# Another order of the first instructions of a fused attention and SwiGLU kernel

## The chip, the cores and the metric

The kernel runs on one core of one Trainium2 chip. The metric is the device time of one execution in microseconds (us), lower is better; the number before is the median of five runs.

## The reference

Attention with normalised queries and keys over 8 sequences and 12 heads of 448 tokens and 64 columns, and then a SwiGLU feed-forward block over the 3584 x 768 matrix that the heads make side by side:

```python
def rmsnorm(x, g):
    return x / np.sqrt(np.mean(x * x, axis=-1, keepdims=True) + 1e-06) * g
q_n, k_n = rmsnorm(q, g_q), rmsnorm(k, g_k)
scores = np.matmul(q_n, k_n.transpose(0, 1, 3, 2)) / np.sqrt(64)
attn = softmax(scores)                        # over the keys
x = np.matmul(attn, v)                        # (8, 12, 448, 64) -> (3584, 768)
xn = rmsnorm(x, rms_g)
g, val = xn @ w_gate, xn @ w_val              # 768 x 1536 each
out = (g * sigmoid(g) * val) @ w_out          # 1536 x 768
```

## The kernel before, in words

**Pairs.** Two heads make a pair; there are 6 pairs for each sequence and 48 in all, and pair `g` is the unit of the attention part. The 448 tokens of a head are cut into three blocks of 128 (`FULL`, handled as [128 partitions, 3 blocks]) and 64 last ones, the *rest*. The rests of all 12 heads of a sequence lie in one tile `rest`: queries in 64 of its partitions, keys in the other 64.

**One pair.** `load_pair` brings q in one DMA and k in two into the tile `qk`; `load_rests` brings the rests' queries (i = 0) or keys (i = 1) in two DMAs each. `squares(g, i)` squares the queries (i = 0) or keys (i = 1) on ScalarE (ACT, L478) and sums them by row on VectorE (DVE, L481). `rms_qk` makes the reciprocal roots on GpSimd (POOL): an addition (L497) and a power (L498). `norm_q` scales the queries into the tile `qn` (L503, two instructions). The keys are not scaled; their root goes into the exponential as a scale by row. `norm_rests(b, lo, hi)` does the same for the rests of pairs lo to hi: square on ACT (L446), sum on DVE (L448), root on POOL (L453, L454), scale (L458).

`turn(g, 0)` transposes the queries on TensorE (PE, L519, three instructions) and the rest tile (L523), and copies the result to `qT` with ACT (L524) and to the last 64 columns of `kT` with DVE (L525). `turn(g, 1)` transposes the keys (L519) and copies them to the first 384 columns of `kT` with DVE (L527). `score(g, cs)` multiplies (L537) and takes exponentials on ACT (L541) for the key blocks in `cs`, `rests(g)` for the rest keys (L567, L582). `values(g)` makes the products with v in the PSUM bank `av` (L573, L589), `sums(g)` the softmax denominators: for the first seven pairs directly on PE (L578, L602), followed by a reciprocal (L606, 2.95 us) and the product `x` (L617) on DVE. `av` has a single bank, so that the next pair's L573 follows this pair's L617.

**Weights.** They come as 64-bit numbers and are made 32-bit ones piece by piece: `convert()` moves each piece one step on, with a load on SP's queue (L719), a split on ACT (L728, L729), a join on DVE (L734, L735, L736; called a conversion below), an addition on POOL (L773) and a store (L761). Conversions start with the second pair. From about 100 us on the feed-forward products fill PE beside the attention of the next sequences.

**The order.** It is written out by hand: each engine and each DMA queue takes its instructions in the order in which the Python code issues them, and semaphores hold an instruction until its inputs are there. `pe(fn)` issues a block of PE work and counts it; `after(n, fn)` puts other work on a list, to be issued when n more blocks have been counted:

```python
def pe(fn):
    now["t"] += 1
    fn()
    for item in [d for d in due if d[0] <= now["t"]]:
        due.remove(item)
        item[1]()
```

Work that falls due at the same block is issued in the order in which it was put on the list. `warm(n)` issues n products of the identity with itself, whose result nothing reads; each shows as two records in the trace.

Of the kernel before, what the change touches and what calls it, by code (L numbers as in the profile page):

```python
# [8 lines left out]
F32 = mybir.dt.float32  # L9
# [3 lines left out]
ALU = mybir.AluOpType  # L13
ACT = mybir.ActivationFunctionType
AX_X = mybir.AxisListType.X
# [3 lines left out]
B, H, S, D = 8, 12, 448, 64  # L19
DM, DF = H * D, 1536  # L20
NT, P = 4, 112
NK, REST = 3, S - 3 * 128
# [313 lines left out]
def safe_scores(  # L336
# [20 lines left out]
    nc = tc.nc  # L357

    def pool(name, bufs, **kw):
        return ctx.enter_context(tc.tile_pool(name=name, bufs=bufs, **kw))  # L360
# [3 lines left out]
    qk_pool, v_pool, qn_pool, qkT_pool = pool("c_qk", 4), pool("c_v", 3), pool("c_qn", 1), pool("c_qkT", 2)  # L364
# [9 lines left out]
    st = {}  # L374
# [4 lines left out]
    def after(n, fn):  # L379
        due.append((now["t"] + n, fn))  # L380
# [7 lines that stand above are left out]
# [12 lines left out]

    FULL, LAST = slice(0, NK * 128), slice(NK * 128, S)

    def load_pair(g):

        if g >= NG:
            return
        b, hp = divmod(g, NPAIR)
        qk = st["qk", g] = qk_pool.tile([128, 2, 2 * NK * D], F32, name="qk")
        nc.sync.dma_start(out=qk[:, 0].rearrange("p (h n) -> p h n", h=2),
                          in_=q[b, 2 * hp:2 * hp + 2, FULL].rearrange("h (p t) d -> p h (t d)", t=NK))  # L410
        for h in range(2):
            nc.sync.dma_start(out=qk[:, 1].rearrange("p (t h d) -> p h t d", h=2, d=D)[:, 1 - h],
                              in_=k[b, 2 * hp + h, FULL].rearrange("(p t) d -> p t d", t=NK))

# [9 lines left out]
    def load_rests(b, i, engine):  # L424
        if b >= B:
            return
        if i == 0:
            st["rest", b] = rest_pool.tile([128, NPAIR, 2, D], F32, name="rest")
        for h in range(2):
            engine.dma_start(out=st["rest", b][own(i), :, 1 - h], in_=(q, k)[i][b, h::2, LAST].rearrange("h i d -> i h d"))  # L430
# [8 lines left out]
    def norm_rests(b, lo, hi):  # L439

        if b >= B:
            return
        n = hi - lo
        rest = st["rest", b][:, lo:hi]
        sq = tmp.tile([128, n, 2, D], F32, name="sq", tag="sq", bufs=2)
        nc.scalar.activation(sq, rest, ACT.Square)  # L446
        ms = small.tile([128, n, 2], F32, name="msr")
        after(1, lambda: nc.vector.tensor_reduce(out=ms, in_=sq, axis=AX_X, op=ALU.add))  # L448

        first = b == lo == 0  # L450

        def root():
            nc.gpsimd.tensor_scalar(ms, ms, D * 1e-6, None, ALU.add)  # L453
            nc.gpsimd.tensor_tensor(ms, ms, mhalf[:, 0:2 * n].rearrange("p (n h) -> p n h", h=2), ALU.pow)  # L454

        def scale():

            (nc.vector if first else nc.gpsimd).tensor_tensor(rest, rest, ms.unsqueeze(3).to_broadcast([128, n, 2, D]), ALU.mult)  # L458

        after(1 if b == 0 else 2, root)  # L460
        if first:
            return scale
        after(1 if b == 0 else 2, scale)

    def direct(g):
# [3 lines left out]
    def squares(g, i):  # L469

        if g >= NG:
            return
        n = 2 * NK
        if i == 0:
            st["ms", g] = small.tile([128, 2 * n], F32, name="ms")
        ms = st["ms", g]
        sq = tmp.tile([128, n * D], F32, name="sq", tag="sq", bufs=2)
        nc.scalar.activation(sq, st["qk", g][:, i], ACT.Square)  # L478

        def reduce():  # L480
            nc.vector.tensor_reduce(out=ms[:, i * n:(i + 1) * n], in_=sq.rearrange("p (n d) -> p n d", d=D), axis=AX_X, op=ALU.add)  # L481

        after(1, reduce)
        if g <= 1:

            after(1, lambda: rms_qk(g, slice(i * n, (i + 1) * n)))
            if i == 0:
                after(1, lambda: norm_q(g))
        elif i == 1:
            after(2, lambda: rms_qk(g))  # L490
            after(2, lambda: norm_q(g))

    def rms_qk(g, cols=slice(0, 4 * NK)):
        if ("rs", g) not in st:
            st["rs", g] = small.tile([128, 4 * NK], F32, name="rs")
        ms = st["ms", g][:, cols]
        nc.gpsimd.tensor_scalar(ms, ms, D * 1e-6, None, ALU.add)  # L497
        nc.gpsimd.tensor_tensor(st["rs", g][:, cols], ms, mhalf[:, cols], ALU.pow)  # L498

    def norm_q(g):  # L500
        qn = st["qn", g] = qn_pool.tile([128, 2 * NK * D], F32, name="qn")
        for h in range(2):
            (nc.vector if g <= 1 else nc.gpsimd).tensor_tensor(  # L503
                qn.rearrange("p (t h d) -> p h t d", h=2, d=D)[:, 1 - h], st["qk", g][:, 0].rearrange("p (h t d) -> p h t d", h=2, d=D)[:, h],
                st["rs", g][:, h * NK:(h + 1) * NK].unsqueeze(2).to_broadcast([128, NK, D]), ALU.mult)

# [669 lines left out]
        todo.extend(items + (out_items(b) if b == B - 1 else []))  # L1176


    load_pair(0)
    load_rests(0, 0, nc.scalar)  # L1180
    load_rests(0, 1, nc.sync)
    load_pair(1)
    ident = const.tile([128, 128], F32, name="ident")
    make_identity(nc, ident)
# [20 lines left out]
    def gains():  # L1205


        nc.vector.scalar_tensor_tensor(gqk, gq, D**0.5, gk, ALU.mult, ALU.mult)
        nc.vector.tensor_scalar(gqk, gqk, SAFE, -SAFE, ALU.min, ALU.max)
# [28 lines left out]
            convert()  # L1238


    squares(0, 0)
    warm(9)
    pe(idle)
    scale = norm_rests(0, 0, 2)
    squares(0, 1)
    after(1, scale)
    pe(lambda: turn(0, 1))
    gains()
    squares(1, 0)
    squares(1, 1)  # L1250
    warm(5)
    pe(lambda: turn(0, 0))
    for g in range(NG + 1):
        b, hp = divmod(g, NPAIR)
        if g:
            load_pair(g + 3)
        if hp == 2:
            for i in range(2):
                load_rests(b + 1, i, nc.sync)
            load_v_rests(b + 1)  # L1260
        if g == 0:
            pe(lambda: score(0, (0,)))
            pe(lambda: rests(0))
            pe(lambda: score(0, (1, 2)))
            pe(lambda: turn(1, 0))
            squares(2, 0)
            squares(2, 1)
            pe(lambda: turn(1, 1))
            norm_rests(0, 2, 4)
            for _ in range(3):  # L1270
                convert()
            load_pair(3)
            load_v(2)
            convert()
            load_rows()
            continue
        if g <= NPAIR:
            pe(lambda: score(g, (0,)))
            squares(g + 2, 0)
            squares(g + 2, 1)  # L1280
            turns(g < NPAIR)
            if g > 1:
                pe(lambda: turn(g + 1, 0))
                some_rests(g)
                pe(lambda: turn(g + 1, 1))
            pe(lambda: rests(g))
            pe(lambda: values(g - 1))
            if g == 1:
                pe(lambda: turn(g + 1, 0))
                some_rests(g)  # L1290
                pe(lambda: turn(g + 1, 1))
            load_v(g + 2)
            turns(g < NPAIR)
            pe(lambda: sums(g - 1))
            pe(lambda: score(g, (1, 2)))
            turns(1 if g < NPAIR else 3)
            if g == 2:
                bound()
            continue

        pe(lambda: (rests(g), score(g, (0,)) if g < NG else None))
        if g == NPAIR + 1:
            pe(lambda: rms_x(0))
        pe(lambda: values(g - 1))
        load_v(g + 2)
        if g == NPAIR + 1:
            pe(lambda: score(g, (1,)))
            pe(lambda: norm_x(0))
            pe(lambda: score(g, (2,)))
        pe(lambda: sums(g - 1))  # L1310
        if g == NPAIR + 1:
            begin(0, 15)
        elif g < NG:
            pe(lambda: score(g, (1, 2)))
        st["block"] = now["t"]
        if hp:
            fill()
            squares(g + 2, 0)
            squares(g + 2, 1)
            pe(lambda: turn(g + 1, 0))  # L1320
            some_rests(g)
            fill()
            pe(lambda: turn(g + 1, 1))
            fill()
            continue
        fill(3)
        pe(lambda: turn(g + 1, 0))
        fill(1)
        pe(lambda: rms_x(b - 1))
        squares(g + 2, 0)  # L1330
        squares(g + 2, 1)
        pe(lambda: turn(g + 1, 1))
        fill(len(todo))
        begin(b - 1, 16)
        pe(lambda: norm_x(b - 1))
        fill()
# [41 lines left out]
```

## Time and profile before

| | |
|---|---|
| median of 5 runs | 1604.63 us (1603.41 to 1605.05) |
| the profiled execution | 1601.5 us |
| its span, first to last instruction | 1599.7 us |
| PE busy | 1572.5 us, 98% |
| DVE, POOL, ACT busy | 879.4, 658.8, 469.9 us |
| granted TensorE clock | 0.999 |

A row of the order of time reads: start in us, length in us, engine, line of the kernel, operation, output <- input, shapes, how many instructions were merged, and in brackets the idle time of the engine ahead of it with what ended it. PEld is TensorE's loading of weights, SPq the DMA queue of SyncE. A row of busy time by stretches reads: start:end, length, busy time of the engine with the number of instructions, granted TensorE clock, share of the DMA engines, GB/s. The lengths of PE's records are modelled, and records of one engine overlap a little; sums are therefore made from start to start where an instruction follows another.

### The profile page before, as it was taken

The page shows a single profiled execution, that of the slowest core. Times are in us where ns is not written, and L with a number is a line of the kernel's source. Part 1 is how long each engine was busy: PE and PEld are TensorE (multiplying, and loading weights), DVE is VectorE, ACT ScalarE, POOL GpSimd, SP SyncE. Part 2 cuts the span into 40 slices and gives each one's busy share as a digit, 9 for nine tenths or more (in the row PEclk, how much of TensorE's full clock was granted, in tenths as well). Part 3 has the DMA queues.
Part 4 walks back from the last instruction along what each step waited for, and adds up shares of the span by engine and source line. Part 5 has one row for each costly group of instructions (what it writes and reads, how often), then busy time and mean ns, then how long its engine had stood idle before and what let it go on. Part 6 is the DMA issues. An engine that isn't in the chain of part 4 may idle for free.

```text
span 1599.7 us, 21577 instructions
## 1 busy us (share of the span) xinstructions
PE 1572.5 (98%) x7286; PEld 1114.3 (70%) x7286; DVE 879.4 (55%) x1553; ACT 469.9 (29%) x940; POOL 658.8 (41%) x715
## 2 busy tenths in 40 slices
PE   8999999999999999999999999999999999999998
PEld 4344445687756887568875788667885688859974
DVE  5989899578833556325562354635563355513531
ACT  6746464232222222222222222323322222101010
POOL 7867877465424443343433443344542342000000
PEclk9999999999999999999999999999999999999999
DMA  7648574866756554465544755584553544457652
GB/s 216 199 139 264 165 242 134 278 196 222 250 160 195 154 150 134 134 202 153 155 122 137 208 154 154 149 261 129 163 149 124 173 141 136 124 167 218 174 150 60
DMA packets 261996, 273.28 MB, mean 171 GB/s; under 512 B 78836, under 2 KB 258804, under 8 KB 261876
## 3 DMA queue, kind: packets, MB, share of 16 engines
q1 hardware_dynamic: 260948, 271.61, 56.6%
q8 instruction: 60, 0.98, 0.3%
q14 instruction: 60, 0.49, 0.1%
q10 hardware_dynamic: 800, 0.20, 0.1%
q0 software_dynamic: 128, 0.00, 0.0%
HBM read 232.40 MB, written 39.32 MB: 170 GB/s over the span
## 4 chain that ended last, share of the span: by engine, by line
PE 79%; DVE 7%; issue 1%; POOL 0%; DMA 0%; ACT 0%; SPq 0%; DVEq 0%; POOLq 0%
PE ff L889 40%; PE ff L1079 22%; PE sc L537 6%; PE av L589 5%; PE sc L567 2%; PE den L602 2%; PE tr L519 1%; DVE top L735 1%; DVE top L736 1%; DVE top L734 1%; PE ff L989 1%; DVE rd L610 1%; DVE h L912 0%; DVE h L911 0%; DVE w L846 0%
## 5 line engine op out<-in xcount | busy, mean ns | idle before, releaser
L889 PE MATMUL ff<-x,w 128*128 128x224 f32 x1878 | 381.5, 354 | 4.4 <-DVE h L912 2.6
L889 PEld LDWEIGHTS ff<-x,w 128*128 128x128 f32 x1878 | 351.3, 190 | 20.0 <-issue 11.1
L547 POOL TENSOR_TENSOR es<-e 128x448 f32<-128x448 f32 x82 | 91.6, 1138 | 495.3 <-ACT e L541 495.3
L889 PE MATMUL ff<-xs,w 128*128 128x224 f32 x1374 | 281.7, 353 | 3.3 <-DVE w L846 3.3
L889 PEld LDWEIGHTS ff<-xs,w 128*128 128x128 f32 x1374 | 258.0, 190 | 7.1 <-issue 6.0
L554 POOL TENSOR_TENSOR es<-es,e 64x448 f32<-64x448 f32 (+1 forms) x164 | 191.8, 1180 | 6.3
L610 DVE RECIPROCAL rd<-rd 128x448 f32<-128x448 f32 x41 | 121.0, 2952 | 110.5 <-ACT rd L609 110.5
L541 ACT ACTIVATE e<-sc,rs 128x448 f32<-128x448 f32 x288 | 161.6, 634 | 48.0 <-PE sc L537 45.6
L1079 PE MATMUL ff<-w,h 128*128 128x384 f32 x498 | 167.8, 487 | 0.6 <-ACT p L1058 0.6
L1079 PE MATMUL ff<-w,raw 128*128 128x384 f32 x468 | 159.5, 487 | 0.3 <-DVE y L1051 0.3
L537 PE MATMUL sc<-qT,kT 64*128 64x448 f32 x576 | 138.4, 572 | 3.4 <-ACT sq L478 1.8
L1079 PEld LDWEIGHTS ff<-w,h 128*128 128x128 f32 x498 | 93.5, 190 | 64.5 <-issue 1.3
L1079 PEld LDWEIGHTS ff<-w,raw 128*128 128x128 f32 x468 | 87.6, 190 | 60.9 <-issue 2.6
L589 PE MATMUL av<-e,vt 128*64 128x448 f32 x576 | 118.8, 548 | 0.0
L498 POOL TENSOR_TENSOR rs<-ms,mhalf 128x12 f32<-128x12 f32 (+1 forms) x50 | 114.2, 2283 | 4.2
L537 PEld LDWEIGHTS sc<-qT,kT 64*128 64x128 f32 x576 | 54.4, 185 | 84.4 <-issue 68.3
L1107 PE MATMUL ff<-x,w 128*128 128x448 f32 x288 | 111.8, 541 | 0.0
L901 DVE TENSOR_TENSOR cc<-ff,u 128x448 f32<-128x448 f32 x84 | 52.4, 623 | 91.8 <-PE ff L889 91.6
L773 POOL TENSOR_TENSOR w<-top,raw 128x384 int32<-128x384 int32 x72 | 77.4, 1088 | 36.5 <-DVE top L736 20.0
L589 PEld LDWEIGHTS av<-e,vt 128*64 128x64 f32 x576 | 37.1, 136 | 75.6 <-issue 74.9
L1107 PEld LDWEIGHTS ff<-x,w 128*128 128x128 f32 x288 | 53.3, 190 | 50.8 <-issue 49.0
L623 POOL TENSOR_TENSOR ss<-ss,rd 128x448 f32<-128x448 f32 x40 | 46.9, 1172 | 79.5 <-ACT rd L622 79.5
(127 smaller groups left out, 1809.9 us busy)
## 6 DMA issues: line engine op xcount, KB each, us to landing
w<-kept SPq DMA_DIRECT2D x511, 192.0 KB, 2.7
w<-kept_o SPq DMA_DIRECT2D x296, 192.0 KB, 2.7
kept<-w SPq DMA_DIRECT2D x89, 192.0 KB, 3.9
qk<-in_q_dram SPq DMA_DIRECT2D x48, 192.0 KB, 3.1
qk<-in_k_dram SPq DMA_DIRECT2D x96, 96.0 KB, 3.5
vt<-in_v_dram SPq DMA_DIRECT2D x48, 192.0 KB, 2.5
raw<-in_moe_w_gate_dram SPq DMA_DIRECT2D x24, 384.0 KB, 4.5
raw<-in_moe_w_val_dram SPq DMA_DIRECT2D x24, 384.0 KB, 4.8
```

Of the source, the lines that this page charges most:

```text
L498: nc.gpsimd.tensor_tensor(st["rs", g][:, cols], ms, mhalf[:, cols], ALU.pow)
L537: nc.tensor.matmul(ps[:, 0:S], lhsT=kT[r, c * 128:(c + 1) * 128], rhs=qT[r, :], start=True, stop=True)
L541: nc.scalar.activation(e, ps[:, 0:S], ACT.Exp, scale=rs[:, n:n + 1])
L547: nc.gpsimd.tensor_tensor(es, st["e", g, 0, j], st["e", g, 1, j], ALU.add)
L554: nc.gpsimd.tensor_tensor(es[r], es[r], e[r], ALU.add)
L589: nc.tensor.matmul(av[own(j), 0:S], lhsT=vt[:, j, c], rhs=st["e", g, c, j], start=False, stop=(c == NK - 1), skip_group_check=True)
L610: nc.vector.reciprocal(rd, rd)
L773: nc.gpsimd.tensor_tensor(data(key).bitcast(I32), top, lo, ALU.add)
L889: nc.tensor.matmul(bank[:, w * HT:(w + 1) * HT], lhsT=wt[:, c * 128:(c + 1) * 128], rhs=x[:, c, :], start=onto is None and w == c == 0, st ...
L901: nc.vector.tensor_tensor(add[name], ps[:, 0:S], add[other], ALU.add)
L1079: nc.tensor.matmul(ps, lhsT=left_o(b, which, LEFT_O[name], c), rhs=data(("wo", b, name, c)), start=first and c == 0, stop=c == NFP - 1, sk ...
L1107: nc.tensor.matmul(bank[w][:, 0:S], lhsT=data(key)[:, c * 128:(c + 1) * 128], rhs=st["x", 0, half][:, c, :], start=half == c == 0, stop=ha ...
```

## The change

Only the order of the first three pairs and the engine of two of their steps change; nothing that is computed changes.

- **Loads.** On SP's queue the keys of the first rests go ahead of the first pair's k (two DMAs each). The queries of the rests stay on ACT's queue.
- **First steps.** `squares` of pairs 0 and 1 and `norm_rests(0, 0, 2)` hand back their sum and root, and these are issued by name where they stand, no longer by the list. VectorE's order becomes: sum of q0, `norm_q(0)`, sum of the rests, copy of the keys (L527), sum of k0, scale of the rests, gains, sum of q1, copy of the rest keys (L525), sum of k1, `norm_q(1)`. An empty `pe(idle)` goes.
- **First scores.** `score(0, (1, 2))` is cut in two, and `turn(1, 0)` stands between them. The number of counted blocks is the same as before, so that everything later falls due at the same places.
- **Third pair.** `norm_q(2)` moves from POOL to DVE, and so does the scaling of the rests of pairs 2 and 3 (L458).

```diff
--- before.py
+++ after.py
@@ -400,15 +400,17 @@
 
     FULL, LAST = slice(0, NK * 128), slice(NK * 128, S)
 
-    def load_pair(g):
+    def load_pair(g, parts=(0, 1)):
 
         if g >= NG:
             return
         b, hp = divmod(g, NPAIR)
-        qk = st["qk", g] = qk_pool.tile([128, 2, 2 * NK * D], F32, name="qk")
-        nc.sync.dma_start(out=qk[:, 0].rearrange("p (h n) -> p h n", h=2),
-                          in_=q[b, 2 * hp:2 * hp + 2, FULL].rearrange("h (p t) d -> p h (t d)", t=NK))
-        for h in range(2):
+        if 0 in parts:
+            qk = st["qk", g] = qk_pool.tile([128, 2, 2 * NK * D], F32, name="qk")
+            nc.sync.dma_start(out=qk[:, 0].rearrange("p (h n) -> p h n", h=2),
+                              in_=q[b, 2 * hp:2 * hp + 2, FULL].rearrange("h (p t) d -> p h (t d)", t=NK))
+        qk = st["qk", g]
+        for h in range(2) if 1 in parts else ():
             nc.sync.dma_start(out=qk[:, 1].rearrange("p (t h d) -> p h t d", h=2, d=D)[:, 1 - h],
                               in_=k[b, 2 * hp + h, FULL].rearrange("(p t) d -> p t d", t=NK))
 
@@ -445,21 +447,24 @@
         sq = tmp.tile([128, n, 2, D], F32, name="sq", tag="sq", bufs=2)
         nc.scalar.activation(sq, rest, ACT.Square)
         ms = small.tile([128, n, 2], F32, name="msr")
-        after(1, lambda: nc.vector.tensor_reduce(out=ms, in_=sq, axis=AX_X, op=ALU.add))
-
+        reduce = lambda: nc.vector.tensor_reduce(out=ms, in_=sq, axis=AX_X, op=ALU.add)
         first = b == lo == 0
+
+        engine = nc.vector if b == 0 and lo < 4 else nc.gpsimd
 
         def root():
             nc.gpsimd.tensor_scalar(ms, ms, D * 1e-6, None, ALU.add)
             nc.gpsimd.tensor_tensor(ms, ms, mhalf[:, 0:2 * n].rearrange("p (n h) -> p n h", h=2), ALU.pow)
 
         def scale():
-
-            (nc.vector if first else nc.gpsimd).tensor_tensor(rest, rest, ms.unsqueeze(3).to_broadcast([128, n, 2, D]), ALU.mult)
-
+            engine.tensor_tensor(rest, rest, ms.unsqueeze(3).to_broadcast([128, n, 2, D]), ALU.mult)
+
+        if first:
+            reduce()
+            root()
+            return scale
+        after(1, reduce)
         after(1 if b == 0 else 2, root)
-        if first:
-            return scale
         after(1 if b == 0 else 2, scale)
 
     def direct(g):
@@ -480,13 +485,11 @@
         def reduce():
             nc.vector.tensor_reduce(out=ms[:, i * n:(i + 1) * n], in_=sq.rearrange("p (n d) -> p n d", d=D), axis=AX_X, op=ALU.add)
 
+        if g <= 1:
+
+            return reduce, lambda: rms_qk(g, slice(i * n, (i + 1) * n))
         after(1, reduce)
-        if g <= 1:
-
-            after(1, lambda: rms_qk(g, slice(i * n, (i + 1) * n)))
-            if i == 0:
-                after(1, lambda: norm_q(g))
-        elif i == 1:
+        if i == 1:
             after(2, lambda: rms_qk(g))
             after(2, lambda: norm_q(g))
 
@@ -500,7 +503,7 @@
     def norm_q(g):
         qn = st["qn", g] = qn_pool.tile([128, 2 * NK * D], F32, name="qn")
         for h in range(2):
-            (nc.vector if g <= 1 else nc.gpsimd).tensor_tensor(
+            (nc.vector if g <= 2 else nc.gpsimd).tensor_tensor(
                 qn.rearrange("p (t h d) -> p h t d", h=2, d=D)[:, 1 - h], st["qk", g][:, 0].rearrange("p (h t d) -> p h t d", h=2, d=D)[:, h],
                 st["rs", g][:, h * NK:(h + 1) * NK].unsqueeze(2).to_broadcast([128, NK, D]), ALU.mult)
 
@@ -1176,9 +1179,10 @@
         todo.extend(items + (out_items(b) if b == B - 1 else []))
 
 
-    load_pair(0)
+    load_pair(0, (0,))
     load_rests(0, 0, nc.scalar)
     load_rests(0, 1, nc.sync)
+    load_pair(0, (1,))
     load_pair(1)
     ident = const.tile([128, 128], F32, name="ident")
     make_identity(nc, ident)
@@ -1238,18 +1242,26 @@
             convert()
 
 
-    squares(0, 0)
+    def at_once(steps):
+        for step in steps:
+            step()
+
+    at_once(squares(0, 0))
     warm(9)
-    pe(idle)
+    norm_q(0)
     scale = norm_rests(0, 0, 2)
-    squares(0, 1)
-    after(1, scale)
+    steps = squares(0, 1)
     pe(lambda: turn(0, 1))
+    at_once(steps)
+    scale()
     gains()
-    squares(1, 0)
-    squares(1, 1)
+    at_once(squares(1, 0))
+    reduce, root = squares(1, 1)
     warm(5)
     pe(lambda: turn(0, 0))
+    reduce()
+    norm_q(1)
+    root()
     for g in range(NG + 1):
         b, hp = divmod(g, NPAIR)
         if g:
@@ -1261,8 +1273,9 @@
         if g == 0:
             pe(lambda: score(0, (0,)))
             pe(lambda: rests(0))
-            pe(lambda: score(0, (1, 2)))
+            pe(lambda: score(0, (1,)))
             pe(lambda: turn(1, 0))
+            pe(lambda: score(0, (2,)))
             squares(2, 0)
             squares(2, 1)
             pe(lambda: turn(1, 1))
```

## The prediction

> **What bounds the kernel now.** I read the page first, then busy time by stretches, then the order of time of each engine over the first 100 us.
>
> ```profile
> span 1599.7 us, 21577 instructions
> PE 1572.5 (98%) x7286; PEld 1114.3 (70%) x7286; DVE 879.4 (55%) x1553; ACT 469.9 (29%) x940; POOL 658.8 (41%) x715
> ```
>
> PE is idle for 27 us in all, so no order of instructions can bring more, and the change reaches only what runs before about 35 us. PE's own order of time has three pauses at the places that are edited:
>
> ```profile
> 10.00 0.33 PE L523 MATMUL tr<-ident,rest 128*128 128x128 f32 x1 [1.10 <-DVE rest L458]
> 17.56 1.02 PE L537 MATMUL sc<-qT,kT 64*128 64x448 f32 x4 [1.82 <-ACT sq L478]
> 24.29 0.33 PE L523 MATMUL tr<-ident,rest 128*128 128x128 f32 x1 [1.16 <-POOL rest L458]
> ```
>
> They are 4.08 us together. But from 25 us on another engine has no room either. Busy time of VectorE by stretches (start:end, length, busy):
>
> ```profile
> 20.00:25.00 5.00, 1.19 (x3) 1.00 0.54 158
> 25.00:30.00 5.00, 4.61 (x7) 1.00 0.97 264
> 30.00:40.00 10.00, 9.76 (x16) 1.00 0.67 187
> 50.00:60.00 10.00, 9.83 (x12) 1.00 0.66 194
> 70.00:80.00 10.00, 9.79 (x14) 1.00 0.69 212
> ```
>
> VectorE is idle from 21.72 to 25.32 and then works without a gap until the key sums at 72.6. Its rows where that begins:
>
> ```profile
> 18.36 0.42 DVE L448 TENSOR_REDUCE msr<-sq 128x4 f32<-128x256 f32 x1
> ...
> 25.32 0.23 DVE L525 COPY kT<-tr 128x64 f32<-128x64 f32 x1 [3.61 <-ACT qT L524]
> 25.46 0.55 DVE L527 COPY kT<-tr 128x384 f32<-128x384 f32 x1
> 25.93 0.41 DVE L448 TENSOR_REDUCE msr<-sq 128x4 f32<-128x256 f32 x1
> 26.26 0.35 DVE L734 TENSOR_SCALAR top<-top 128x384 f32<-128x384 f32 x1
> 26.64 0.36 DVE L735 TENSOR_SCALAR top<-top 128x384 int32<-128x384 int32 x1
> 27.04 0.56 DVE L736 SCALAR_TENSOR_TENSOR top<-raw,top 128x384 int32<-128x384 int32 x1
> 27.51 2.95 DVE L606 RECIPROCAL rd<-den 128x448 f32<-128x448 f32 x1
> 30.50 0.62 DVE L617 TENSOR_TENSOR x<-av,rd 128x448 f32<-128x448 f32 x1
> ```
>
> The first reciprocal follows a conversion at once, although its sums on PE were through at 27.36. Its product x ends at 31.12; PE's next `av` (L573), which needs that bank free, starts at 31.42. That slack is 0.30, then 41.87 - 41.70 = 0.17, and at 52.84 PE comes straight behind x (52.69). So **what counts is when VectorE reaches the first reciprocal**, not PE's pauses. VectorE's wait at 84.52 (2.42, for PE's sums) goes back the same way: PE had waited 1.38 for POOL's `qn`, which had waited for VectorE's key sums at 72.6. From 100 us PE is full, and a shift stays to the end.
>
> **First edit, the loads.** The key rests' two DMAs go from 2.63 to 1.25 on SP's queue, the first k pair from 1.25 to 2.56 (their own 1.31 later); what follows keeps its place. From issue to first use the rows give 4.42 (k, used at 5.67) and 4.54 (rests, at 7.17). So the rests can be used at 5.7 to 5.8, k at 7.0 to 7.1. On VectorE the rests' sum now stands behind `norm_q(0)`: 7.06 to 7.48; root on POOL 1.45 (8.04 to 9.49); scale 8.96 to 9.39, against 9.95 before. On PE the key transposes start 1.35 later, and what stands in order from them (transposes, five warm, three transposes, five warm) took 5.67 to 8.90 = 3.23 in a row: 10.2 to 10.3. So the rest transpose starts not at 10.00 but at about 10.2: **+0.2**, ends -0.55 (scale alone decides) and +0.4. The gain of the earlier rests is spent by the later k. PE also pauses 1.5 us ahead of the key transposes. If it then ran slow, as its first 18 records did (4.21 / 18 = 0.234 each, against 1.28 / 10 = 0.128), the 20 warm records would cost 2.1. After the 1.82 pause at 17.56 four scores took 1.02, as many as at 11.05, so I take 0 and keep 2.1 for a rival.
>
> **Second edit, turn(1, 0) ahead of the last scores.** ACT works from 13.96 to 17.52 without a gap: four exponentials, qT, two squares. qT goes ahead of two exponentials; the sum is the same, so the squares start at 16.56 + 0.2. VectorE's copies of kT no longer wait for qT at 16.73: PE's key transposes end near 16.1, the copy near 16.7, and score(1) starts at about 16.75 in place of 17.56. The queries' sum for pair 2 had waited for the copies (17.33, with its square through at 17.06): 0.25 regained. The 12-column root of pair 2 on POOL, which ended at 21.06, thus ends at P = 21.06 - 0.25 + 0.2 = 21.0. Also moved are `norm_q(1)` and the sums of pair 1: root of q1 from about 11.0 to 12.4, so qn(1) is there near 13.1, and PE takes it near 14. That costs nothing; if this cover were gone, its 0.63 would show.
>
> **Third edit, pair 2's scaling on VectorE.** This adds a wait. In the due list `norm_q(2)` stands ahead of the rests' sum (L448), and now both are on VectorE. Before, that sum ran at 18.36, then a conversion (18.80 to 20.18) and pair 3's sums (20.71 to 21.72), all under POOL's root:
>
> ```profile
> 18.76 2.30 POOL L498 TENSOR_TENSOR rs<-ms,mhalf 128x12 f32<-128x12 f32 x1
> 21.14 0.97 POOL L503 TENSOR_TENSOR qn<-qk,rs 128x192 f32<-128x192 f32 x2
> 22.19 0.23 POOL L453 TENSOR_SCALAR msr<-msr 128x4 f32<-128x4 f32 x1
> 22.51 1.04 POOL L454 TENSOR_TENSOR msr<-msr,mhalf 128x4 f32<-128x4 f32 x1
> 23.62 0.61 POOL L458 TENSOR_TENSOR rest<-rest,msr 128x256 f32<-128x256 f32 x1
> ```
>
> Now VectorE stands still from 18.3 to P, and behind it queue the rests' sum, their scale (which must wait for POOL a second time), the first conversion and pair 3's sums; ACT's second square of pair 3 waits for the rests' sum as well (a buffer of two), and gets through before qT(2). In start-to-start times: `norm_q` 0.58 (6.48 to 7.06), sum 0.42, root and its hand-overs 1.48 (8.04 to 9.52): scale at P + 2.48 = 23.5. It takes 0.43, so PE's rest transpose starts at 23.97 in place of 24.29: 0.32 gained on PE. VectorE goes on with scale 0.34, conversion 1.25 (26.26 to 27.51), pair 3's sums 0.92 (35.46 to 36.38), and the five rows from 25.32 to 27.51, 2.19. The reciprocal starts at P + 2.48 + 0.34 + 1.25 + 0.92 + 2.19 = P + 7.18 = 28.2, against 27.51: **+0.68**. VectorE's 3.6 us of idle time have moved ahead of work that they used to follow.
>
> POOL loses 0.97 + 0.61, but its root for pair 3 now waits for sums that end at P + 5.08 = 26.1 (21.72 before). Root from 26.5 (2.39), `qn` 0.97, root and scale of the next rests 2.04 (22.19 to 24.23) put its three weight additions (L773) at 32.0, not 30.51. There they meet conversions 2 and 3. A conversion's L735 takes 0.36 alone and 1.06 beside an addition; these two took 31.04 to 35.33 = 4.29 with the additions partly beside x, and 52.61 to 58.68 = 6.07 where all three fell beside them. So 0 to +1.78; I take **+0.4**, near the lower end, because the third addition still waits for conversion 2, as at 33.58. A gain here is excluded: the additions cannot move earlier.
>
> [...] Conversion 1 will lie beside POOL's root for pair 3 (about 26.5 to 28.9); the same three instructions lay beside pair 2's root at 18.80 and took 0.38, 0.36 and 0.56, as alone, so I add nothing. [...]
>
> **The sum.** 0.68 + 0.4 = +1.1 (the +0.2 and -0.25 are in P). The span goes from 1599.7 to 1600.8, the profiled execution from 1601.5 to 1602.6. The median of the runs shown lies 3.1 above that execution, and I carry the difference: 1604.63 + 1.1 = **1605.7**.
>
> **The rivals.**
> - *VectorE is not the bound* (B): its delay is taken up by slack, and all three pauses of PE go: -4.08, 1600.5. For it: each pause is named by a row. Against it: the 97% rows, and slack of at most 0.30 at x. In a weak form only the 0.32 at 24.29 remains: 1604.3.
> - *The additions collide in more pairs* (C, slower): POOL, later than before, puts its three additions back to back beside two conversions in pairs 1 and 2 too, as the trace shows from 52.61. Price 1.78 each: 0.68 + 3.56 = +4.2, 1608.9. It decides once more than 2.5 us of collisions are added. Against it: POOL idles 1.95 ahead of 36.55 and restarts on VectorE's sums, so the pairs fall into step again.
> - *PE falls slow in its longer first pause* (D): 2.1 + 1.1 = +3.2, 1607.8.
>
> **How the numbers follow.** A measurement of this kernel tells about 0.2% (3.2 us) from no change: 1601.4 to 1607.8. The forecast has 0.66, B 0.10 and its weak form 0.08, C 0.13, D 0.03, on the edge. Forecast, weak B and half of D are within 0.2%, less some 0.01 of tail: 0.75; slower 0.15; faster 0.10. The terms' ends give -0.1 to +2.7; a collision of 1.78 in a later pair can come or go. With part of B and C the range is 1602.3 to 1608.3.
>
> **What would show it.** Right: L458 of pairs 2 and 3's rests on DVE near 23.5 behind an idle DVE from 18.3 to 21; first L606 near 28.2; PE's L523 pauses at about 10.2 and 24.0, no long pause ahead of 16.75; `av` (L573) waiting for x near 31.8. Wrong: L606 at or before 27.5, k used before 6.5, or DVE gaps between 30 and 70.

## The result and the profile after

Over 28 runs the changed kernel's median is 1605.28 us, that of the kernel before over 48 runs beside them 1603.43: a ratio of 1.0014 [1.0009, 1.0019], or +1.85 us. This is inside the 0.2% that count as no change, and inside the range. The five runs shown at first had put the kernel before 1.2 higher, at 1604.63; so the forecast *difference*, +1.1, was 0.75 too low, and the forecast time, 1605.7, only 0.4 too high. That the time came so near is partly luck: a start that was too high made up for a change that was put too low.

The profiled execution after took 1607.1 us. From its page:

```profile
span 1605.3 us, 21576 instructions
PE 1577.7 (98%) x7286; PEld 1117.5 (70%) x7286; DVE 881.6 (55%) x1556; ACT 470.0 (29%) x940; POOL 656.4 (41%) x712
```

VectorE's busy time by stretches (start:end, length, busy) is as before: little up to 25 us, then no room.

```profile
20.00:25.00 5.00, 0.95 (x3) 1.00 0.58 144
25.00:30.00 5.00, 4.72 (x13) 1.00 1.00 295
30.00:40.00 10.00, 9.81 (x13) 1.00 0.53 138
50.00:60.00 10.00, 9.79 (x14) 1.00 0.61 187
70.00:80.00 10.00, 9.83 (x13) 1.00 0.75 223
```

Line numbers are 2 to 5 higher now: the scale of the rests is L460, the sums L486, `norm_q` L506, key copies L528 and L530, conversions L737 to L739, reciprocal L609, x L620, POOL's additions L776. VectorE's order of time where its work without a gap begins:

```profile
22.71 0.63 DVE L506 TENSOR_TENSOR qn<-qk,rs 128x192 f32<-128x192 f32 x2 [2.76 <-POOL rs L501]
23.25 0.41 DVE L450 TENSOR_REDUCE msr<-sq 128x4 f32<-128x256 f32 x1
25.14 0.43 DVE L460 TENSOR_TENSOR rest<-rest,msr 128x256 f32<-128x256 f32 x1 [1.48 <-POOL msr L457]
25.48 0.35 DVE L737 TENSOR_SCALAR top<-top 128x384 f32<-128x384 f32 x1
...
26.74 1.00 DVE L486 TENSOR_REDUCE ms<-sq 128x6 f32<-128x384 f32 x2
...
29.84 2.95 DVE L609 RECIPROCAL rd<-den 128x448 f32<-128x448 f32 x1
32.83 0.62 DVE L620 TENSOR_TENSOR x<-av,rd 128x448 f32<-128x448 f32 x1
33.37 0.49 DVE L737 TENSOR_SCALAR top<-top 128x384 f32<-128x384 f32 x1
33.89 1.05 DVE L738 TENSOR_SCALAR top<-top 128x384 int32<-128x384 int32 x1
34.98 1.25 DVE L739 SCALAR_TENSOR_TENSOR top<-raw,top 128x384 int32<-128x384 int32 x1
...
48.16 1.37 DVE L739 SCALAR_TENSOR_TENSOR top<-raw,top 128x384 int32<-128x384 int32 x1
```

The two new waits stand there, 2.76 and 1.48, and behind them the conversion and pair 3's sums. The first reciprocal is at 29.84 and was at 27.51. The next ones are at 40.89 and 52.68 (38.10 and 49.09 before): the distances grew by 0.46 and 0.80. From then on the shift stays: 3.59 at the third reciprocal, 3.58 at 88.10 against 84.52, and 3.58 when PE reaches its product `msx` (94.42 against 90.84), the last mark used below. TensorE's order of time shows a part that the change's own waits did not make:

```profile
7.11 0.87 PE L522 MATMUL tr<-ident,qk 128*128 128x128 f32 x3 [1.54 <-DMA qk<-in_k_dram]
7.77 2.34 PE L1230 MATMUL warm<-ident 128*128 128x128 f32 x10
9.90 0.84 PE L522 MATMUL tr<-ident,qn 128*128 128x128 f32 x3
10.54 1.48 PE L1230 MATMUL warm<-ident 128*128 128x128 f32 x10
11.86 0.27 PE L526 MATMUL tr<-ident,rest 128*128 128x128 f32 x1
12.86 1.02 PE L540 MATMUL sc<-qT,kT 64*128 64x448 f32 x4 [0.72 <-ACT qT L527]
...
18.49 1.02 PE L540 MATMUL sc<-qT,kT 64*128 64x448 f32 x4 [0.74 <-ACT e L544]
...
25.62 0.33 PE L526 MATMUL tr<-ident,rest 128*128 128x128 f32 x1 [1.56 <-DVE rest L460]
```

Of PE's three pauses the first is gone, but 1.54 now stand ahead of the key transposes; the second fell from 1.82 to 0.74, the third grew to 1.56. But ten warm records took 2.34 and not 1.28: PE still ran at half pace here (the trace's first record of a granted clock, 1.0, starts at 10.97), and the first score came at 12.86 instead of 11.05. PE runs at half pace again at about 407 us (start:end, length, PE busy, granted clock):

```profile
403.50:406.91 3.41, 1.55 (x9) 1.00 0.83 284
406.91:410.32 3.41, 3.41 (x11) 0.50 0.97 274
410.32:413.73 3.41, 3.41 (x22) 1.00 0.97 341
```

One such stretch cost 1.65 to 1.7 us where it fell between 8 and 12 us or between 370 and 410 us, and 1.2 us where it fell between 74 and 82 us (the shift behind it against the shift ahead of it, both against the kernel before). The runs of one kernel fall into groups: the 48 before lie at about 1601.6 (8 runs), 1603.3 (23) and 1604.8 (17); those after at 1603.6 (2), 1605.1 (15), 1606.8 (10), and one at 1609.3. The three kernels whose profile holds no such stretch and none of the third edit's engine changes took 1601.4 to 1601.5 in the profiled execution, so the lowest group is read as the one without stretches; that reading is not shown run by run. Group against group the change costs 1.9 to 2.0. Below, therefore, each experiment gets its median ratio, and the marks of its profile are read with the half-pace stretches ahead of the last mark named.

Another part of the cost lies at the very end. VectorE's last rows, before and after, are

```profile
1593.16 0.56 DVE L1051 TENSOR_TENSOR y<-ff,cc 128x384 f32<-128x384 f32 x1 [3.31 <-PE ff L1079]
```

```profile
1598.44 0.56 DVE L1054 TENSOR_TENSOR y<-ff,cc 128x384 f32<-128x384 f32 x1 [3.31 <-PE ff L1082]
```

and from their start to the end of the span it is 6.55 before and 6.87 after. The same holds below: 6.55 in every kernel whose engines are those of before, 6.87 to 7.08 in every kernel with a part of the third edit's engine changes. Behind that row the profile shows only the last stores and the end of the program; why that part grows stays open.

### The profile page after: what moved, and what is told of

It reads as the page before. It is cut to its first block, busy times and chain, and to the rows that moved or that the text cites. A ratio compares the mean times of both kernels' runs of the same rounds, so it can differ in the third digit from the quotient of the medians.

```text
span 1605.3 us, 21576 instructions
## 1 busy us (share of the span) xinstructions
PE 1577.7 (98%) x7286; PEld 1117.5 (70%) x7286; DVE 881.6 (55%) x1556; ACT 470.0 (29%) x940; POOL 656.4 (41%) x712
## 4 chain that ended last, share of the span: by engine, by line
PE 79%; DVE 7%; issue 1%; POOL 0%; DMA 0%; ACT 0%; SPq 0%; DVEq 0%; POOLq 0%
PE ff L892 40%; PE ff L1082 22%; PE sc L540 6%; PE av L592 5%; PE sc L570 2%; PE den L605 2%; PE tr L522 1%; DVE top L738 1%; DVE top L739 1%; DVE top L737 1%; PE ff L992 1%; DVE rd L613 1%; DVE h L915 0%; DVE h L914 0%; DVE w L849 0%
## 5 line engine op out<-in xcount | busy, mean ns | idle before, releaser
L776 POOL TENSOR_TENSOR w<-top,raw 128x384 int32<-128x384 int32 x72 | 77.1, 1085 | 36.5 <-DVE top L739 20.3
L904 DVE TENSOR_TENSOR u<-ff,p 128x448 f32<-128x448 f32 x42 | 26.1, 622 | 96.8 <-PE ff L892 96.8
```

Source lines behind the costliest of these rows:

```text
L776: nc.gpsimd.tensor_tensor(data(key).bitcast(I32), top, lo, ALU.add)
L904: nc.vector.tensor_tensor(add[name], ps[:, 0:S], add[other], ALU.add)
```

## The experiments

Edit 1 is the loads and the first steps, edit 2 the first scores, edit 3 the third pair. The theory: what costs is VectorE's order in edit 3, and collisions with POOL that follow from it. The rivals: the later k of edit 1 costs; or VectorE has slack and the clock explains it all. Marks: first score / first reciprocal / spacing of reciprocals 1 to 2 and 2 to 3 / `msx`. Before: 11.05 / 27.51 / 10.59, 10.99 / 90.84. After: 12.86 / 29.84 / 11.05, 11.79 / 94.42.

### The edits one by one

**Edit 1 alone** (the changed kernel with edits 2 and 3 undone; the empty block keeps the count):

```diff
-        engine = nc.vector if b == 0 and lo < 4 else nc.gpsimd
+        engine = nc.vector if first else nc.gpsimd
-            (nc.vector if g <= 2 else nc.gpsimd).tensor_tensor(
+            (nc.vector if g <= 1 else nc.gpsimd).tensor_tensor(
     warm(9)
+    pe(idle)
-            pe(lambda: score(0, (1,)))
+            pe(lambda: score(0, (1, 2)))
             pe(lambda: turn(1, 0))
-            pe(lambda: score(0, (2,)))
```

> Edit 1 alone (loads and first steps; turn(1, 0) and pair 2's scaling as before). Reference points of the two profiles, before and after: first score 11.05 and 12.86, first reciprocal 27.51 and 29.84, the sums `msx` 90.84 and 94.42. Queue theory (VectorE held behind norm_q(2) is the lasting cost): no VectorE wait of 2.8 near 20; if PE is at full pace, first score near 11.25, first reciprocal near 27.7, msx near 91.0, median within 0.5 us of before. Clock theory (PE stays slow after its 1.5 us pause, and that belongs to edit 1): key transposes 0.87 long, ten warm records 2.3 long, first score near 12.8, reciprocal near 29.2, median +1.5. Third theory (all of the cost is the later k): median +1.9 and msx at 94.4.

Measured: 1604.07, ratio 1.0006 [0.9997, 1.0014]; 12.72 / 29.18 / 10.59, 10.97 / 92.49. Its lowest runs, 1601.35, equal those of before. Spacings are as before; the shift of 1.65 at `msx` is one half-pace stretch, from 8.24 to 11.66, just behind a PE pause of 1.90. That edit 1 costs nothing at full pace is shown only by the fourth experiment.

**Edit 2 alone** (in the kernel before):

```diff
-            pe(lambda: score(0, (1, 2)))
+            pe(lambda: score(0, (1,)))
             pe(lambda: turn(1, 0))
+            pe(lambda: score(0, (2,)))
```

> Edit 2 alone (turn(1, 0) ahead of the last scores, in the kernel before). Queue theory: score(1) starts near 16.6 and not 17.56, pair 2's root ends 0.25 earlier (20.8), so rest scale, first reciprocal (27.26) and msx (90.6) all 0.25 earlier; median 0 to -0.4 us. Theory that PE's pauses are the bound: reciprocal and msx 0.8 earlier, median -0.8.

Measured: 1603.52, ratio 1.0001 [0.9992, 1.001]; 10.95 / 27.53 / 10.59, 10.98 / 90.83. score(1) starts at 16.93 in place of 17.56, but the reciprocal doesn't move. The turn waited 0.28 for `qn`, ACT waited once more for PE's scores (0.20), and the squares of pair 2 started at 16.79, not before 16.56. PE's pause shrank from 1.82 to 0.74, the next one grew from 1.16 to 1.58, and the path that counts did not move.

**Edit 3 alone** (in the kernel before, with both engines changed):

```diff
-            (nc.vector if first else nc.gpsimd).tensor_tensor(rest, ...
+            (nc.vector if b == 0 and lo < 4 else nc.gpsimd).tensor_tensor(rest, ...
-            (nc.vector if g <= 1 else nc.gpsimd).tensor_tensor(
+            (nc.vector if g <= 2 else nc.gpsimd).tensor_tensor(
```

> Edit 3 alone (norm_q(2) and the scale of the rests of pairs 2 and 3 on VectorE, in the kernel before). Queue theory: VectorE stands still from about 18.4 to 21.1; P = 21.06; rest scale at P + 2.48 = 23.54, PE's rest transpose 0.3 earlier, first reciprocal at P + 7.18 = 28.24 (+0.73), collisions of additions and conversions +0.46 at pair 1 and +0.8 at pair 2 as in the changed kernel, msx +2.0 at 92.8; median +1.5 to +2.2. Rival (edit 3 costs nothing, the later k does it all): reciprocal and msx as before or 0.3 earlier, median 0 to -0.4.

Measured: 1606.85, ratio 1.002 [1.001, 1.0031]; 11.32 / 30.09 / 11.04, 11.80 / 94.70. The spacings are those of the changed kernel. A half-pace stretch from 11.72 to 15.14 is in the 30.09.

**Edits 1 and 2 without 3** (the changed kernel with only the engines put back):

> Edits 1 and 2 without edit 3 (pair 2's scaling on POOL again). Queue theory: no VectorE wait behind norm_q(2); first reciprocal 6.45 after the end of pair 2's root (7.16 in the changed kernel), no added collisions; median about 2.0 below the changed kernel at the same pace of PE, so about 0 to -0.2 against before, or +1.5 if PE stays slow in its first 10 us. Rival (the later k does it all): median as the changed kernel, +1.9.

Measured: 1602.9, ratio 0.9999 [0.999, 1.0007]; 11.02 / 27.29 / 10.58, 10.98 / 90.61. This profile ran at full pace throughout. In TensorE's order of time the same pause of 1.54 is followed by warm records of normal length:

```profile
7.11 0.52 PE L522 MATMUL tr<-ident,qk 128*128 128x128 f32 x3 [1.54 <-DMA qk<-in_k_dram]
7.46 1.28 PE L1230 MATMUL warm<-ident 128*128 128x128 f32 x10
...
11.02 1.02 PE L540 MATMUL sc<-qT,kT 64*128 64x448 f32 x4 [0.72 <-ACT qT L527]
```

So at full pace edit 1 moves the first score by -0.03. Together with it edit 2 does bring what it promised: the turn no longer waits for `qn`, pair 2's root ends at 18.54 + 2.30 = 20.84 in place of 21.06, and the reciprocal is 0.22 earlier, again 6.45 behind the end of that root. The loss belongs to edit 3.

### Edit 3 taken apart

**Only `norm_q(2)` on VectorE** (in the kernel before, `g <= 1` to `g <= 2` in `norm_q`):

> Half of edit 3 in the kernel before: only norm_q(2) goes to VectorE; the rests of pairs 2 and 3 are still scaled on POOL. VectorE stands still from 18.4 to 21.1 behind norm_q(2), but then nothing else holds it: rests' sum 21.65 to 22.1, POOL's root 22.2 to 23.6 and scale to 24.2 as before, conversion and pair 3's sums done at 24.3, ahead of qT(2). If the lasting cost is VectorE's second wait (for the root of the rests, ahead of the conversion and pair 3's sums): first reciprocal 27.5, msx 90.8 to 91.0, median 0 to +0.2 us. If the cost is the wait behind norm_q(2) itself, as the prediction put it first: reciprocal 28.2, msx 92.8, median +2.

Measured: 1603.85, ratio 1.0003 [0.9994, 1.0012]; 11.12 / 27.65 / 10.58, 10.99 / 90.96. VectorE's order of time:

```profile
21.17 0.63 DVE L503 TENSOR_TENSOR qn<-qk,rs 128x192 f32<-128x192 f32 x2 [2.76 <-POOL rs L498]
21.71 0.41 DVE L448 TENSOR_REDUCE msr<-sq 128x4 f32<-128x256 f32 x1
22.04 0.35 DVE L734 TENSOR_SCALAR top<-top 128x384 f32<-128x384 f32 x1
...
25.46 0.23 DVE L525 COPY kT<-tr 128x64 f32<-128x64 f32 x1 [1.16 <-ACT qT L524]
...
27.65 2.95 DVE L606 RECIPROCAL rd<-den 128x448 f32<-128x448 f32 x1
```

The wait of 2.76 is the changed kernel's, and costs next to nothing on this path (0.12 at `msx`): the work queued behind it is through by 24.3, and 1.16 of idle time remain before the key copy at 25.46. The median's +0.45 agrees with the later end: 7.00 from VectorE's last row to the end of the span.

**Only the scale of the rests on VectorE** (in the kernel before):

```diff
-            (nc.vector if first else nc.gpsimd).tensor_tensor(rest, ...
+            (nc.vector if b == 0 and lo < 4 else nc.gpsimd).tensor_tensor(rest, ...
```

> The other half of edit 3 in the kernel before: only the scale of the rests of pairs 2 and 3 goes to VectorE. The rests' sum runs at 18.4 as before, and then VectorE stands still until POOL has done root (to 21.06), norm_q(2) and the rests' root (to 23.55): scale at 23.58, then conversion, pair 3's sums, copies; first reciprocal 23.58 + 4.70 = 28.3 (+0.8), pair 3's sums end at 26.2 and not 21.7, POOL's additions 1.5 later and so beside the conversions, msx near 92.9, median +2. If the cost is the wait behind norm_q(2) itself: reciprocal 27.5 or earlier, median 0.

Measured: 1606.11, ratio 1.002 [1.0011, 1.0029]; 11.16 / 28.39 / 11.05, 11.81 / 93.00. VectorE's order of time:

```profile
18.46 0.42 DVE L448 TENSOR_REDUCE msr<-sq 128x4 f32<-128x256 f32 x1
23.69 0.43 DVE L458 TENSOR_TENSOR rest<-rest,msr 128x256 f32<-128x256 f32 x1 [4.80 <-POOL msr L454]
24.03 0.35 DVE L734 TENSOR_SCALAR top<-top 128x384 f32<-128x384 f32 x1
...
25.29 1.01 DVE L481 TENSOR_REDUCE ms<-sq 128x6 f32<-128x384 f32 x2
```

One instruction of 0.43 us holds VectorE for 4.80 us, and the conversion and pair 3's sums, which had filled that time, come after it. The reciprocal is 0.88 later, the spacings add 0.46 and 0.82: 2.16 together, and `msx` is 2.16 later, at full pace up to that mark. The end adds 0.45 (7.00). So this one instruction makes the whole loss of edit 3 up to `msx`.

### Putting the order right

**`norm_q(2)` and the scale behind the first conversion** (in the changed kernel):

```diff
-        after(1 if b == 0 else 2, scale)
+        after(2 if b or lo == 2 else 1, scale)
-            after(2, lambda: norm_q(g))
+            after(3 if g == 2 else 2, lambda: norm_q(g))
```

> The changed kernel with VectorE's queue in another order: rests' sum, then the conversion, then norm_q(2) and the scale of the rests, one block later than now. Nothing that is ready waits behind norm_q(2). If the order of that queue is the cause of the loss: norm_q(2) at 20.9, POOL's root of the rests done at 22.3, scale 22.35 to 22.8, PE's rest transpose near 22.9 and not 24.3, first reciprocal near 26.1 (27.51 before), msx near 89.4, median about -1.4 us against before and -3.4 against the changed kernel (PE at full pace; a slow stretch of PE's clock adds about 1.6 to any run). If the engines themselves are the cause (VectorE has no room for the two steps): msx 92 to 93, median +1 to +2.

Measured: 1604.65, ratio 1.0001 [0.9992, 1.001]; 12.42 / 27.57 / 11.07, 11.85 / 93.47. The reciprocal is as early as before although the first score was 1.37 late (half pace until 10.25). The reciprocal and the spacings make 1.40 at `msx`; the other 1.23 is a half-pace stretch at 78.52. The spacings are still those of the changed kernel: pair 3's sums stand behind the scale, so POOL's root for pair 3 is still late.

**Both behind pair 3's sums too**:

```diff
-        after(1 if b == 0 else 2, scale)
+        after(3 if b == 0 and lo == 2 else 1 if b == 0 else 2, scale)
-            after(2, lambda: norm_q(g))
+            after(4 if g == 2 else 2, lambda: norm_q(g))
```

> The changed kernel with VectorE's queue as before up to pair 3's sums, and norm_q(2) and the scale of the rests only behind them (rests' sum, conversion, pair 3's sums, norm_q(2), scale). The order tried before gained on the first reciprocal, but pair 3's sums still stood behind the scale, POOL started its root for pair 3 1.0 later than before, and its additions fell beside conversions (+0.5 at pair 1 and +0.8 at pair 2). If that lateness of POOL is the cause of the collisions: POOL's root for pair 3 starts right behind the rests' root (near 22.8; 24.65 before), additions end ahead of the conversions of pair 1, first reciprocal near 26.1 at full pace of PE, x to x 10.6 and then 11.0 as in the kernel before (11.05 and 11.8 in the changed one), msx near 89.4, fastest runs 1.4 us below the fastest of before. If the collisions come by themselves once VectorE is early: x to x 11.05 and 11.8, msx near 90.7, as before.

Measured: 1602.06, ratio 0.9996 [0.9987, 1.0005]; 12.44 / 27.63 / 10.39, 10.98 / 90.75, the first score again late by half pace until 10.31. VectorE's order of time, then POOL's:

```profile
21.93 1.01 DVE L486 TENSOR_REDUCE ms<-sq 128x6 f32<-128x384 f32 x2 [0.54 <-ACT sq L483]
22.85 0.62 DVE L506 TENSOR_TENSOR qn<-qk,rs 128x192 f32<-128x192 f32 x2
23.74 0.42 DVE L460 TENSOR_TENSOR rest<-rest,msr 128x256 f32<-128x256 f32 x1 [0.27 <-POOL msr L457]
```

```profile
24.36 2.30 POOL L501 TENSOR_TENSOR rs<-ms,mhalf 128x12 f32<-128x12 f32 x1
...
30.16 2.01 POOL L776 TENSOR_TENSOR w<-top,raw 128x384 int32<-128x384 int32 x2
```

The waits of 2.76 and 1.48 have become 0 and 0.27, and the reciprocal starts 5.36 behind the end of pair 2's root (19.97 + 2.30), against 6.45 before and 7.16 in the changed kernel: measured from there, it is earlier than before whatever PE's pace ahead of it. Pair 3's root starts at 24.36 (28.17 in the changed kernel, 24.65 before), the additions at 30.16 (33.60 and 30.51), and the spacings are back at 10.39 and 10.98. What decides is how far that root starts ahead of the first reciprocal: 2.9 us before and with `norm_q(2)` alone, 3.3 here, and the spacings do not grow; 1.7 in the changed kernel and with the scale alone, 1.9 in the order tried first, and both spacings grow. The collisions were thus the work of POOL's late root for pair 3.

### The pause ahead of the key transposes

**Fourteen warm products ahead of the key transposes, none behind them**, first with both instructions behind the first conversion, then with both behind pair 3's sums too:

```diff
-    warm(9)
+    warm(14)
...
-    warm(5)
     pe(lambda: turn(0, 0))
```

> As the run before, and the warm products moved: 14 ahead of the key transposes in place of 9, none between the key and the query transposes. PE then has no 1.5 us pause ahead of the keys, and the rest transpose is no longer held by warm products: it starts when the rests are scaled, 9.4 to 9.5, first score near 10.5. Queue theory: everything 0.5 earlier than in the run before, first reciprocal near 25.6, msx near 88.9, median about -1.9 against before. If the first scores are not on the path: as the run before.

Measured: 1601.49, ratio 0.9992 [0.9983, 1.0001]; 10.49 / 25.72 / 11.07, 11.83 / 91.59. The reciprocal is 1.79 earlier than before, the collisions give 0.48 + 0.84 back, and a half-pace stretch at 76.64 costs 1.22 more: `msx` is 0.75 late.

> As the run before, with 14 warm products ahead of the key transposes and none between key and query transposes. First score near 10.5, first reciprocal near 25.6, and without the collisions of the earlier run of this kind msx near 89.0, fastest runs 1.8 below the fastest of before, median about -1.9. If the collisions come by themselves: msx near 90.3, fastest runs within 0.5 of before.

Measured: 1601.89, ratio 0.9992 [0.9983, 1.0001]; 10.50 / 25.76 / 10.40, 10.97 / 90.05. Two half-pace stretches, at 74.79 and 402.47, are in this profile; the first costs 1.17 at `msx`. These two kernels, measured on different chips, were then not told apart by their medians, although the lowest times differ by 1.3 (1600.01 and 1601.30).

### Again, beside each other

> The changed kernel itself once more, for a profile with another course of PE's clock. In its first profile PE ran at half pace until 10.6 us and once more near 403 us. If that is chance and no part of the change: it comes or not, and with PE at full pace the first score starts near 11.05, first reciprocal near 28.0, x to x 11.05 and 11.8 again, msx near 92.8 (+2.0 against before). If the half pace belongs to the change (its 1.5 us pause of PE): first score near 12.8, first reciprocal near 29.8, msx near 94.4 again.

Measured: 1605.21, ratio 1.0013 [1.0004, 1.0022]; 12.49 / 29.48 / 11.06, 11.79 / 94.07. Once more half pace until 10.26, and for one stretch from 406.21.

> The last kernel once more beside the two others on one chip, for its interval: first reciprocal near 25.8, x to x 10.4 and 11.0, fastest runs near 1600.0 (before 1601.5, the changed kernel 1603.5), median 1 to 1.5 below before and 3 to 3.5 below the changed kernel.

Measured: 1600.07, ratio 0.9984 [0.9975, 0.9993]: 3.2 below the kernel before beside it (1603.3), 5.1 below the changed one. 10.52 / 25.74 / 10.38, 10.98 / 88.85, at full pace throughout, span 1598.2. TensorE's order of time, then a row of VectorE's:

```profile
7.16 0.52 PE L522 MATMUL tr<-ident,qk 128*128 128x128 f32 x3 [0.64 <-DMA qk<-in_k_dram]
...
10.52 1.02 PE L540 MATMUL sc<-qT,kT 64*128 64x448 f32 x4 [0.75 <-ACT qT L527]
```

```profile
25.74 2.94 DVE L609 RECIPROCAL rd<-den 128x448 f32<-128x448 f32 x1
```

The pause is 0.64 instead of 1.54, the first score 0.53 and the reciprocal 1.77 earlier than before. `msx` is 1.99 earlier, and the lowest run 1.57 below that of before: the later end (7.04 against 6.55) takes the difference back. So the three edits, with the two VectorE instructions behind the work that is ready and the warm products in one piece, gain 0.16%: inside the 0.2% that count as no change, but with an interval clear of 1. The order without the warm products (1602.06) has a gain in its lowest runs only; by its median it is not shown.

## Why the prediction was right, and where it was off

| step | put | measured |
|---|---|---|
| first score, edit 1 | +0.2 | -0.03 at full pace, +1.81 in the profile after |
| end P of pair 2's root, edit 2 | -0.25 | +0.02 alone, -0.22 with edit 1 |
| scale of the rests, edit 3 | P + 2.48 | 22.68 + 2.46 = 25.14 |
| PE's rest transpose | P + 2.97 | P + 2.94 = 25.62 |
| first reciprocal | P + 7.18 | P + 7.16 = 29.84 |
| POOL's additions | P + 11.0 | P + 10.92 = 33.60 |
| collisions | +0.4 | +0.46 and +0.80 |
| end of the program | nothing | +0.32 |
| in all | +1.1 | +1.85 by medians, 1.9 to 2.0 group against group |

At full pace the measured terms add up to 2.07: -0.22 from edits 1 and 2, 7.16 - 6.45 = 0.71 from edit 3's chain, 0.46 + 0.80 from the collisions, 0.32 at the end. In edit 1 the +0.2 came from putting key transposes, warm products and query transposes at 3.23 in a row; start to start they took 7.11 to 10.02 = 2.91 in the profile of edits 1 and 2 without 3.

**The bound** held. VectorE has no room from 25 us on, the first reciprocal sets what follows, and its shift, with that of the spacings, carries to `msx` to within 0.03, but for the three profiles with a half-pace stretch at 74.79, 76.64 or 78.52, which adds 1.2. The rival that VectorE is not the bound is out: edit 2 alone took PE's pause of 1.82 down to 0.74 and gave 0.01 at `msx`, while moving VectorE's two instructions moved the reciprocal from 7.16 to 5.36 behind pair 2's root.

**Edit 3's chain** was right to 0.02 from end to end, by start-to-start times of rows of before. Its *cause* was not told apart. The prediction named two waits of VectorE, from 18.3 to P for `norm_q(2)` and then a second one for the scale, and laid the loss on both; the first costs next to nothing alone (+0.12 at `msx`), the second alone costs 2.16. What decides is whether the ready work still ends before the key copy of 25.3: behind the first wait it does, behind the second not.

**The collisions** were the mis-sized term, 0.4 where 1.26 was measured. In pair 1 the estimate was right: conversions 2 and 3 took 33.37 to 38.12 = 4.75, before 4.29. The further 0.80 is in pair 2, which the prediction had ruled out with the argument that POOL falls into step again at VectorE's sums. In the kernel before, VectorE's and POOL's orders of time have there

```profile
45.38 0.56 DVE L736 SCALAR_TENSOR_TENSOR top<-raw,top 128x384 int32<-128x384 int32 x1
```

```profile
45.73 1.20 POOL L623 TENSOR_TENSOR ss<-ss,rd 128x448 f32<-128x448 f32 x1 [1.00 <-ACT rd L622]
```

and after, where POOL's

```profile
47.79 1.32 POOL L626 TENSOR_TENSOR ss<-ss,rd 128x448 f32<-128x448 f32 x1 [0.29 <-ACT rd L625]
```

is ahead of VectorE's L739 at 48.16, which then takes 1.37. This POOL instruction follows ACT's, not VectorE's sums. ACT and with it POOL came 2.06 later, VectorE 2.78, and so the order of two instructions 0.35 apart turned round. The slower rival (collisions in more pairs) was thus right that one more pair collides, but not by POOL's additions, as it had it, and at 0.80, not 1.78.

**Conversion 1 beside POOL's root**: it ran from 28.59 to 29.93 with 0.35, 0.36 and 0.56, under POOL's 128x12 root of 28.17 to 30.47. The same three rows took 0.35, 0.36 and 0.56 from 25.48 on, where POOL stood idle (25.11 to 27.84). Beside the 128x384 additions L738 and L739 took 1.05 and 1.25 (above). The prediction's choice, nothing added, stands.

**The clock.** The prediction put 2.1 on TensorE being slow behind the longer first pause and gave that 0.03, because four scores behind one other pause had run at full pace. That was too little to go by: of the six profiles with a pause of 1.3 to 1.9 us there, five had half pace in the warm records behind it, which cost 1.4 to 1.8 at the first score; of the eight with at most 0.64, none lost more than 0.3 there. In the timed runs it hardly weighs, for the kernel before loses clock too: in its runs beside the experiments the granted clock was mostly 0.999 near 1601.6, mostly 0.998 near 1603.3 and 0.996 or 0.997 near 1604.8. Its 48 runs lie on average 2.1 above their lowest, the changed kernel's 28 lie 2.3 above theirs. A difference of 0.2 is within the scatter of the runs, so a cost of the pause in the medians is not shown.

## What to carry to other kernels

An engine that takes its instructions in order should get an instruction that waits for another engine only behind all work that is ready: 0.43 us of work in the wrong place cost 2.2 us here. Moved behind the ready work together with `norm_q(2)`, it brought the reciprocal 1.1 us nearer to pair 2's root than it had been before the change. Judge a moved instruction by whether the work behind its wait still ends before the next hard date, not by the length of the wait. And where an instruction takes longer beside another engine's (1.37 in place of 0.56 for VectorE's L739 above), a shift of 2 us can turn round pairs that were 0.35 us apart, far from the edit.

## What the runs showed of the hardware

In the traces before and after, the granted clock changed on a grid of 3.413 us. After the change its record starts with the full clock at 10.97; half of it follows at 406.91, all of it at 410.33 and half again at 1601.58, which is 116.0, 117.0 and 466.0 steps behind the start. In the kernel before it falls to half at 1596.58, 466.0 steps behind its start at 5.97. Between 10.25 and 78.52 of the order tried first lie 20.0 steps, between 10.26 and 406.21 of the changed kernel run again 116.0. The stretch from 406.91 to 410.33 lasted one step at a granted clock of 0.50, and so did that of edit 1 alone, from 8.24 to 11.66.

In the 3.41 us ahead of eleven such stretches PE had paused for 1.37 to 2.13 in all: 1.37 or 1.38 at 74.79, 76.64 and 78.52, 1.82 to 1.86 at six between 370 and 410 us, 1.90 at 8.24 and 2.13 (1.41 + 0.72) at 11.72. The converse doesn't hold: in the kernel before, four steps with 1.38 to 1.71 of pause (from 74.23, 360.95, 388.26 and 398.50) were followed by one at the full clock, and after the change one with 1.44 (from 365.95). What else decides stays open. That the grid is why one kernel's runs fall into groups fits the cost of a stretch, and is not shown.
